# Changing how the first two x tiles and the first weight half reach TensorE in a gated mix of linear and local attention

## The chip, the cores and the metric

The kernel runs on one core of one Trainium2 chip. The metric is the device time of one execution, in microseconds (us); lower is better. A run also carries a mean granted TensorE clock. "Before" is the tuned kernel that the change starts from, "the changed kernel" is the result of the change. Four sets of runs are used, called A to D. In each set both kernels ran on the same chip; sets B, C and D were on three different chips.

## The reference

For x of 2048 rows by 1024 columns, the reference computes a gated sum of two attention blocks:

```
g = sigmoid((x * gate_w).sum(-1))
out = g * A(x) + (1 - g) * B(x)
A: linear attention, 32 heads of 32; phi(t) = where(t > 0, t + 1, exp(t)) + 1e-6 on q and k
B: sliding window of 8 keys, dilation 2, softmax; same shapes
each: qkv = x @ wqkv (1024 x 3072), output @ wo (1024 x 1024)
```

What matters here is only the first product: phi of x times the K columns of A's weights (1024 x 1024), done as two column halves of 512. It contracts over the 1024 columns of x, so TensorE needs x with columns on the partitions, that is, transposed.

## The kernel before

A tile of x is 128 rows (256 KB); there are 16. `xT` is x transposed, `xrow` x as it lies in memory. Tiles 0 and 1 are loaded plain and transposed on TensorE, because TensorE has nothing else to do then. Tiles 2 to 15 are transposed by the DMA crossbar on their way in. The first weight half (1 MB) comes in eight loads on the two issuing engines, SyncE and ScalarE.

```python
load_rows(nc.sync, 0, 1)
load_rows(nc.scalar, 1, 2)
WkA = [wpool.tile([P, KT, 512], BF16, name="WkA0", tag="wa")]
for kt in range(KT):                       # KT = 8
    (nc.scalar if kt % 2 else nc.sync).dma_start(out=WkA[0][:, kt, :], in_=A_wqkv[kt * P:(kt + 1) * P, D:D + 512])
for t in range(2, NB):                     # NB = 16
    nc.sync.dma_start_transpose(out=xT[:, :, t * P:(t + 1) * P], in_=rows(x, t * P, (t + 1) * P))
WkA += load_w("WkA", A_wqkv, D, "wa", only=(1,))
load_rows(nc.sync, 2, 4)
# ... (cut: other weights, constants)
def warm_up(n):
    warm = ps_1.tile([P, P], F32, name="warm", tag="p1")
    for i in range(n):
        nc.tensor.matmul(warm[:], lhsT=onesb[:], rhs=onesb[:], start=True, stop=True)

warm_up(28)
for t in range(2):
    tp = ps_1.tile([P, KT, P], BF16, name="xt_ps", tag="p1")
    for kt in range(KT):
        nc.tensor.transpose(out=tp[:, kt, :], in_=xrow[:, t, kt * P:(kt + 1) * P], identity=ident[:])
    nc.vector.tensor_copy(out=xT[:, 0:4, t * P:(t + 1) * P], in_=tp[:, 0:4, :])
    nc.scalar.copy(out=xT[:, 4:8, t * P:(t + 1) * P], in_=tp[:, 4:8, :])
warm_up(6)
# then tiles 0 and 1 together, 16 matmuls of 128x512, kt by kt; then tiles 2 to 15, 8 matmuls each
```

The warm-up matmuls compute nothing that is used. They keep TensorE busy so that its clock, halved at the start, is released early.

Of the kernel before, what the change touches and what calls it, by code (L numbers as in the profile page):

```python
# [10 lines left out]
BF16 = mybir.dt.bfloat16  # L11
F32 = mybir.dt.float32
PE = mybir.EngineType.PE
DVE = mybir.EngineType.DVE
P = 128
# [26 lines left out]
def kernel(  # L42
# [11 lines left out]
    nc = tc.nc  # L54
    S, D = A_x.shape[1:]
    assert D == 1024 and S == 2048

    x = A_x[0].rearrange("(m two) d -> two m d", two=2)
    out2 = out[0].rearrange("(m two) d -> two m d", two=2)

    def rows(ap, s0, s1):
        return ap[s0 // 1024, s0 % 1024:(s1 - 1) % 1024 + 1, :]
# [3 lines left out]
    KT = D // P  # L66
    NB = S // P
# [10 lines left out]
    big = ctx.enter_context(tc.tile_pool(name="big", bufs=1))  # L78
# [3 lines left out]
    def load_w(name, src, col0, tag, only=(0, 1)):  # L82
        halves = []
        for h in only:
            w = wpool.tile([P, KT, 512], BF16, name=f"{name}{h}", tag=tag)
            c0 = col0 + h * 512
            nc.sync.dma_start(out=w[:], in_=src[:, c0:c0 + 512].rearrange("(kt p) n -> p kt n", p=P))
            halves.append(w)
        return halves

    xT = big.tile([P, KT, S], BF16, name="xT", tag="xT")
    xrow = big.tile([P, NB, D], BF16, name="xrow", tag="vV")

    def load_rows(eng, t0, t1):
        eng.dma_start(out=xrow[:, t0:t1, :], in_=rows(x, t0 * P, t1 * P).rearrange("(t p) d -> p t d", p=P))

    load_rows(nc.sync, 0, 1)
    load_rows(nc.scalar, 1, 2)
    WkA = [wpool.tile([P, KT, 512], BF16, name="WkA0", tag="wa")]
    for kt in range(KT):  # L100
        (nc.scalar if kt % 2 else nc.sync).dma_start(out=WkA[0][:, kt, :], in_=A_wqkv[kt * P:(kt + 1) * P, D:D + 512])
    for t in range(2, NB):
        nc.sync.dma_start_transpose(out=xT[:, :, t * P:(t + 1) * P], in_=rows(x, t * P, (t + 1) * P))
    WkA += load_w("WkA", A_wqkv, D, "wa", only=(1,))
    load_rows(nc.sync, 2, 4)
    for t in range(4, NB, 4):
        load_rows(nc.sync, t, t + 4)
# [35 lines left out]
    def phi(dst, pj):  # L143
        e = work.tile([P, 512], F32, name="e", tag="e")
        nc.scalar.activation(out=e[:], in_=pj[:], func=ACT.Exp)  # L145
        nc.vector.tensor_scalar(out=e[:], in0=e[:], scalar1=1.0, scalar2=1e-6, op0=ALU.min, op1=ALU.add)  # L146
        nc.vector.scalar_tensor_tensor(out=dst, in0=pj[:], scalar=0.0, in1=e[:], op0=ALU.max, op1=ALU.add)

    with tc.manual_schedule(engines={PE}):

        with ExitStack() as s1:
            ps_1 = s1.enter_context(tc.tile_pool(name="ps_1", bufs=6, space=bass.MemoryType.PSUM))
            junk = s1.enter_context(tc.tile_pool(name="junk", bufs=1))


            def warm_up(n):
                warm = ps_1.tile([P, P], F32, name="warm", tag="p1")
                for i in range(n):
                    nc.tensor.matmul(warm[:], lhsT=onesb[:], rhs=onesb[:], start=True, stop=True)

            warm_up(28)
            for t in range(2):
                tp = ps_1.tile([P, KT, P], BF16, name="xt_ps", tag="p1")
                for kt in range(KT):
                    nc.tensor.transpose(out=tp[:, kt, :], in_=xrow[:, t, kt * P:(kt + 1) * P], identity=ident[:])  # L165
                nc.vector.tensor_copy(out=xT[:, 0:4, t * P:(t + 1) * P], in_=tp[:, 0:4, :])
                nc.scalar.copy(out=xT[:, 4:8, t * P:(t + 1) * P], in_=tp[:, 4:8, :])
            warm_up(6)

            s1.enter_context(tc.manual_schedule(engines={DVE}))  # L170
            pk = big.tile([P, NB, D], BF16, name="pk", tag="pkO")
            for half in range(2):
                for t0, n in [(0, 2)] + [(t, 1) for t in range(2, NB)]:
                    pj = [ps_1.tile([P, 512], F32, name="pk_ps", tag="p1") for _ in range(n)]
                    for kt in range(KT):
                        for i in range(n):
                            t = t0 + i
                            nc.tensor.matmul(pj[i][:], lhsT=xT[:, kt, t * P:(t + 1) * P], rhs=WkA[half][:, kt, :],  # L178
                                             start=(kt == 0), stop=(kt == KT - 1))
                    for i in range(n):  # L180
                        phi(pk[:, t0 + i, half * 512:(half + 1) * 512], pj[i])

            zacc = junk.tile([P, D], F32, name="zacc", tag="zacc")
            gw_row = junk.tile([P, D], BF16, name="gw_row", tag="gw")
# [12 lines left out]
            for half in range(2):  # L197
                g_ = kq.tile([P, KT, 512], BF16, name=f"G{half}", tag="kq")
                G.append(g_)
                for kt in range(KT):  # L200
                    pj = ps_1.tile([P, 512], F32, name="g_ps", tag="p1")
                    for t in range(NB):
                        nc.tensor.matmul(pj[:], lhsT=xrow[:, t, kt * P:(kt + 1) * P],  # L203
                                         rhs=pk[:, t, half * 512:(half + 1) * 512],
                                         start=(t == 0), stop=(t == NB - 1))
# [12 lines left out]
            for c in range(KT):  # L218
                kvp = ps_1.tile([P, P], F32, name="kv_ps", tag="p1")
                for kt in range(KT):  # L220
                    nc.tensor.matmul(kvp[:], lhsT=WvA[c // 4][:, kt, (c % 4) * P:(c % 4 + 1) * P],  # L221
                                     rhs=G[c // 4][:, kt, (c % 4) * P:(c % 4 + 1) * P],
                                     start=(kt == 0), stop=(kt == KT - 1))
                nc.vector.tensor_tensor(out=KVT[:, c, :], in0=kvp[:], in1=bdmask[:], op=ALU.mult)
            for half in range(2):
                zp = ps_1.tile([P, 512], F32, name="z_ps", tag="p1")
                for i in range(2):
                    nc.tensor.matmul(zp[:], lhsT=onesb[:], rhs=zhl[:, i, half * 512:(half + 1) * 512],  # L228
                                     start=(i == 0), stop=(i == 1))
# [300 lines left out]
```

## Time and profile before

| | before |
|---|---|
| median of 3 runs | 494.51 us (494.06 to 494.51) |
| span in the profile | 493.0 us |
| first projection matmul | 7.51 us |
| tile 2 starts | 12.39 us |
| tile 2 to the end | 480.6 us |

The first lines of the profile page give the span, and each engine's busy time, share of the span and instructions (PEld is TensorE's weight load):

```profile
span 493.0 us, 8254 instructions
...
PE 487.6 (99%) x3350; PEld 232.0 (47%) x3350; DVE 283.3 (57%) x550; ACT 181.9 (37%) x281; POOL 7.9 (2%) x28
```

TensorE is busy for all but 5.4 us. So a change at the kernel's head can gain time almost only by moving the moment at which TensorE's unbroken stream begins. The chain of waits of the first 20 us, in order of time (start, duration, what), shows what sets that moment:

```profile
...
0.80 4.34 DMA xrow<-in_A_x_dram
5.14 0.05 issue
5.19 1.89 PE xt_ps L165 x16
7.08 0.64 PE warm L159 x6
7.72 12.38 PE pk_ps L178 x51
```

The first 14 us of TensorE on the timeline (start, duration, engine, line, operation, what it writes and reads, count; in brackets the idle time before it and what ended it):

```profile
1.12 3.17 PE L159 MATMUL warm<-onesb 128*128 128x128 bf16 x28 [1.12 <-DVE onesb L117]
5.19 1.89 PE L165 MATMUL xt_ps<-ident,xrow 128*128 128x128 bf16 x16 [0.91 <-DMA xrow<-in_A_x_dram]
6.87 0.85 PE L159 MATMUL warm<-onesb 128*128 128x128 bf16 x6
7.51 6.76 PE L178 MATMUL pk_ps<-WkA_77,xT 128*128 128x512 bf16 x24
```

The warm-ups end at about 4.3 us, x tile 0 lands at 5.14 us, and the projection starts at 7.51 us. At full clock a 128x512 matmul starts every 216 ns. The first seven here start every 427 ns, because the clock is halved until 10.38 us.

A trap for the reader of profiles: the clock record begins with the first release. The table of windows therefore prints a clock of 1.00 for the time before 10.38 us, when the matmuls run at half speed. The matmuls' own spacing has to be read instead.

### The profile page before, as it was taken

What the parts mean: (1) busy time and instruction counts of PE and PEld (TensorE: products, weight loads), DVE (VectorE), ACT (ScalarE), POOL (GpSimd) and SP (SyncE); (2) the same over time, 40 slices, a digit from 0 to 9 for tenths busy, and PEclk for the clock granted to TensorE, in tenths of its full rate; (3) what the DMA queues carried; (4) which work ended last, traced back from release to release, by engine and by line L of the source; (5) the groups of instructions that cost most, each with busy time, mean ns of one, the idle gap of its engine ahead of it and who ended that gap; (6) DMA issues with size and microseconds to landing.
All of it is one profiled execution on the core that took longest, in us unless ns stands there. A gap on an engine that the chain in (4) does not pass through costs nothing.

```text
span 493.0 us, 8254 instructions
## 1 busy us (share of the span) xinstructions
PE 487.6 (99%) x3350; PEld 232.0 (47%) x3350; DVE 283.3 (57%) x550; ACT 181.9 (37%) x281; POOL 7.9 (2%) x28
## 2 busy tenths in 40 slices
PE   8999999999999999999999999999999999999997
PEld 5444444446444444444444545454544444444444
DVE  1766689941328999997476767676765397000000
ACT  1333311121543333332455655655655333112121
POOL 3000000000200000000000000000000000000000
PEclk9999999999999999999999999999999999999999
DMA  8999950000621222236011133111164832110101
GB/s 192 163 277 368 348 167 0 1 0 13 206 76 47 93 93 83 66 122 199 3 36 30 32 88 57 30 36 30 36 134 92 208 85 68 60 43 33 43 33 43
DMA packets 78293, 46.03 MB, mean 93 GB/s; under 512 B 51632, under 2 KB 72240, under 8 KB 78256
## 3 DMA queue, kind: packets, MB, share of 16 engines
q1 hardware_dynamic: 77536, 44.73, 33.6%
q10 hardware_dynamic: 720, 0.79, 0.6%
q8 instruction: 26, 0.43, 0.4%
q14 instruction: 11, 0.09, 0.1%
HBM read 21.23 MB, written 7.34 MB: 58 GB/s over the span
## 4 chain that ended last, share of the span: by engine, by line
PE 98%; DMA 1%; ACT 0%; issue 0%; ACTq 0%
PE kq_ps L339 23%; PE d_ps L458 21%; PE pk_ps L178 11%; PE p_ps L262 11%; PE g_ps L203 11%; PE p_ps L296 8%; PE q_ps L296 2%; DMA xrow<-in_A_x_dram 1%; PE kv_ps L221 1%; PE q_ps_4385 L458 1%; PE q_ps L458 1%; PE p_ps L251 1%; PE xt_ps L165 0%; PE q_ps_4266 L296 0%; PE q_ps_4165 L296 0%; PE z_ps L228 0%
## 5 line engine op out<-in xcount | busy, mean ns | idle before, releaser
L203 PE MATMUL g_ps<-pk,xrow 128*128 128x512 bf16 x256 | 55.4, 379 | 0.0
L146 DVE TENSOR_SCALAR e<-e 128x512 f32<-128x512 f32 x64 | 27.2, 424 | 39.9 <-ACT e L145 39.9
L463 ACT ACTIVATE osb<-d_ps,omg 128x512 bf16<-128x512 f32 (+1 forms) x31 | 20.9, 673 | 72.5 <-PE d_ps L458 64.2
L178 PEld LDWEIGHTS <-xT 128*128 128x128 bf16 x256 | 25.4, 99 | 31.0 <-issue 1.8
L458 PEld LDWEIGHTS <-OBT 128*128 128x128 bf16 x264 | 25.7, 98 | 29.2
L203 PEld LDWEIGHTS <-xrow 128*128 128x128 bf16 x256 | 25.0, 98 | 30.2
L262 PEld LDWEIGHTS <-xT 128*128 128x128 bf16 x256 | 25.0, 98 | 30.2
L296 PEld LDWEIGHTS <-xT 128*128 128x128 bf16 x256 | 24.2, 98 | 28.0
L378 DVE TENSOR_TENSOR PT_1893<-PT_1893,mask 128x672 bf16<-128x672 bf16 (+3 forms) x42 | 23.7, 571 | 18.1 <-ACT PT_1893 L376 17.7
L339 PE MATMUL kq_ps<-xT,WkB_1071 128*128 128x512 bf16 x128 | 32.9, 380 | 0.0
L339 PE MATMUL kq_ps<-xT,WqB_1876 128*128 128x512 bf16 x128 | 32.9, 379 | 0.0
L145 ACT ACTIVATE e<-pk_ps 128x512 f32<-128x512 f32 x32 | 18.9, 597 | 37.9 <-PE pk_ps L178 37.9
L339 PE MATMUL kq_ps<-xT,WkB_1069 128*128 128x512 bf16 x128 | 32.3, 379 | 0.0
L339 PE MATMUL kq_ps<-xT,WqB_1874 128*128 128x512 bf16 x128 | 32.2, 379 | 0.0
L378 DVE TENSOR_TENSOR PT_1894<-PT_1894,mask 128x672 bf16<-128x672 bf16 (+3 forms) x40 | 22.3, 565 | 16.8 <-ACT PT_1894 L376 16.5
L345 DVE CAST kqt<-kq_ps 128x512 bf16<-128x512 f32 x32 | 22.0, 687 | 16.5 <-PE kq_ps L339 16.5
L262 PE MATMUL p_ps<-WvB_114,xT 128*128 128x512 bf16 x128 | 30.9, 379 | 0.0
L262 PE MATMUL p_ps<-WvB_116,xT 128*128 128x512 bf16 x128 | 30.9, 379 | 0.0
L458 PEld LDWEIGHTS <-pqT_4443 128*128 128x128 bf16 x200 | 19.6, 98 | 22.1
L267 ACT CAST tmp<-p_ps 128x512 bf16<-128x512 f32 x32 | 18.8, 587 | 30.3 <-PE p_ps L262 30.3
L178 PE MATMUL pk_ps<-WkA_77,xT 128*128 128x512 bf16 x128 | 29.2, 392 | 0.0
L458 PE MATMUL d_ps<-WoB_4080,OBT 128*128 128x512 bf16 (+1 forms) x128 | 28.5, 366 | 0.0
(399 smaller groups left out, 673.6 us busy)
## 6 DMA issues: line engine op xcount, KB each, us to landing
out_dram<-osb SPq DMA_DIRECT2D x31, 128.0 KB, 1.9
xrow<-in_A_x_dram SPq DMA_DIRECT2D x3, 1024.0 KB, 12.0
pqd<-tmp SPq DMA_DIRECT2D x12, 256.0 KB, 2.0
V<-tmp SPq DMA_DIRECT2D x4, 264.0 KB, 2.5
WkA_100<-in_A_wqkv_dram SPq DMA_DIRECT2D x1, 1024.0 KB, 7.2
WvA_106<-in_A_wqkv_dram SPq DMA_DIRECT2D x1, 1024.0 KB, 14.6
WvA_108<-in_A_wqkv_dram SPq DMA_DIRECT2D x1, 1024.0 KB, 15.3
WoA_110<-in_A_wo_dram SPq DMA_DIRECT2D x1, 1024.0 KB, 13.1
```

The lines of the kernel that those rows point to most:

```text
L145: nc.scalar.activation(out=e[:], in_=pj[:], func=ACT.Exp)
L146: nc.vector.tensor_scalar(out=e[:], in0=e[:], scalar1=1.0, scalar2=1e-6, op0=ALU.min, op1=ALU.add)
L178: nc.tensor.matmul(pj[i][:], lhsT=xT[:, kt, t * P:(t + 1) * P], rhs=WkA[half][:, kt, :], start=(kt == 0), stop=(kt == KT - 1))
L203: nc.tensor.matmul(pj[:], lhsT=xrow[:, t, kt * P:(kt + 1) * P], rhs=pk[:, t, half * 512:(half + 1) * 512], start=(t == 0), stop=(t == NB - 1))
L262: nc.tensor.matmul(st["pj"][:], lhsT=xT[:, kt, t * P:(t + 1) * P], rhs=WvB[half][:, kt, :], start=(kt == 0), stop=(kt == KT - 1))
L267: nc.scalar.copy(out=v[:, half * 16:(half + 1) * 16, 0:Dh], in_=st["pj"][:].rearrange("p (h e) -> p h e", h=16))
L296: nc.tensor.matmul(st["pj"][:], lhsT=xT[:, kt, t * P:(t + 1) * P], rhs=WqA[half][:, kt, :], start=(kt == 0), stop=(kt == KT - 1))
L339: nc.tensor.matmul(st["pj"][:], lhsT=W[c // 4][:, kt, (c % 4) * P:(c % 4 + 1) * P], rhs=xT[:, kt, cols], start=(kt == 0), stop=(kt == KT - 1))
L345: nc.vector.tensor_copy(out=kqt[:, 1, cols], in_=st["pj"][:])
L378: nc.vector.tensor_tensor(out=ptv[:, hs], in0=ptv[:, hs], in1=m[:, None, :].broadcast_to([P, 2, W_]), op=ALU.mult)
L458: nc.tensor.matmul(st["ps"][:, 0:n], lhsT=lhsT, rhs=W[c0 // 512][:, c, c0 % 512:c0 % 512 + n], start=(side == 0 and c == 0), stop=(side == ...
L463: nc.scalar.activation(out=osb[:, 0:n], in_=st["ps"][:, 0:n], func=ACT.Copy, scale=omg[:, tb:tb + 1])
```

## The change

The intent is to start the projection earlier. x tile 0 comes by the crossbar, first on the queue, so that it needs neither TensorE transposes nor copies. The weights come as four quarters on the same queue, with x tile 1 plain between them. The matmuls are put in the order in which their data should arrive. The core of the diff, with lines cut and one line in brackets put for the lines that it names. `project` is one matmul of the projection, `transpose_rows` the eight transposes and two copies of one tile, `phi` the activation that follows:

```diff
-    load_rows(nc.sync, 0, 1)
-    load_rows(nc.scalar, 1, 2)
     WkA = [wpool.tile([P, KT, 512], BF16, name="WkA0", tag="wa")]
-    for kt in range(KT):
-        (nc.scalar if kt % 2 else nc.sync).dma_start(out=WkA[0][:, kt, :], in_=A_wqkv[kt * P:(kt + 1) * P, D:D + 512])
+    nc.sync.dma_start_transpose(out=xT[:, :, 0:P], in_=rows(x, 0, P))
+    for i in range(4):
+        if i == 1:
+            load_rows(nc.sync, 1, 2)
+        nc.sync.dma_start(out=WkA[0][:, 2 * i:2 * i + 2, :],
+                          in_=A_wqkv[2 * i * P:(2 * i + 2) * P, D:D + 512].rearrange("(kt p) n -> p kt n", p=P))
...
     WkA += load_w("WkA", A_wqkv, D, "wa", only=(1,))
+    load_rows(nc.sync, 0, 1)
     load_rows(nc.sync, 2, 4)
...
-            warm_up(28)
-            for t in range(2):
-                (transpose tile t on TensorE, copy it to xT)
-            warm_up(6)
+            warm_up(36)
+            first = [ps_1.tile([P, 512], F32, name="pk_ps", tag="p1") for _ in range(2)]
+            for t, kts in ((0, (0, 1)), ("T", 1), (0, (2, 3)), (1, (0, 1, 2, 3)), (0, (4, 5)), (1, (4, 5)),
+                           (0, (6, 7)), (1, (6, 7))):
+                if t == "T":
+                    transpose_rows(kts)
+                    continue
+                for kt in kts:
+                    project(first[t], t, kt, 0)
+                if kts[-1] == KT - 1:
+                    phi(pk[:, t, 0:512], first[t])
```

From tile 2 on, every computing engine has the same instructions in the same order; SyncE has one load more, the rows of tile 0.

## The prediction

> **What bounds the kernel now.** TensorE is busy 487.6 of 493.0 us (engine table), and the chain of waits is 98% TensorE. From 7.51 us to the end its stream waits for no load; the timeline shows one 128x512 matmul start per 216 ns. So the change can touch only the first 12.4 us, when tiles 0 and 1 of the first projection end (tile 2 starts at 12.39 us). By the timeline they hold: 28 warm-up matmuls from 1.12 to 4.28; 0.91 us idle until the plain load of x tile 0 lands (5.14 us); 16 TensorE transposes and 6 warm-ups at 107 ns (2.3 us); 16 matmuls from 7.51 us, seven at 427 ns because the clock is halved until 10.38 us, nine at 216 ns.
>
> **The clock.** The trace's clock record is halved up to 10.38 us and again from 491.66 us: 481.28 us apart, 141.0 times 3.413 us. That agrees with the free-running 3413 ns window of the Trainium skill ("TensorE: Matmul & The Clock Gate", Part 1). A boundary then lay at 6.97 us; the window before it held the 0.91 us gap and did not release the clock.
>
> **What the change does.**
> - Removes from TensorE 8 transposes and 6 warm-ups after the data (1.5 us at 107 ns), and one PSUM-to-SBUF copy pair (0.42 and 0.58 us). Adds 8 warm-ups before the data, free.
> - Moves: x tile 0 comes by crossbar, first. Issuing a transpose takes 1.31 us of SyncE; landing came 3.9 us after issue at best, under load; issued at 0.8 us, I expect 4.5 to 5.2 us. Weight quarters and x tile 1 follow on one queue, 256 KB each, about 0.7 us each at the 380 GB/s the trace reached: near 5.2 (quarter 0), 5.8 (x1), 6.5, 7.2, 7.9 us. Before, weight rows 5 and 7 landed only at 10.39 and 10.87 us, as their ScalarE issue waited for semaphores until 5.83 us.
> - Crossbar tiles 2 to 15 should flow from about 8 us at 1.4 to 1.55 us each, under the 1.73 us TensorE needs per tile. The second weight half, landing at 34.64 us before (needed near 36.5), should land about 33 us; needed then at 34: little slack.
> - x rows of tile 0 again, 256 KB, needed only at 64 us: free. All other instruction orders are unchanged.
>
> **Sum.** Projection starts near 5.1 us. If gaps stay below about 0.6 us, the clock is released near 7 us: two matmuls and eight transposes halved to 6.9 us, then 14 matmuls at 216 ns: tile 2 starts at 9.9 us instead of 12.4, 2.5 us gained. If the clock is released only at 10.38 us, tile 2 starts at 11.7: 0.7 us. Weight arrival (7.9 us plus four matmuls) caps the gain at about 3.5 us. I allow 0.3 us for later waits. Prediction: gain about 2.0 us, 492.5 us; 8 in 10 between 491.0 and 494.2. Faster by over 2% 0.01, within 2% 0.98, slower by over 2% 0.01.
>
> **Signs.** Right: first projection matmul at 4.8 to 5.5 us; full clock before 8 us; tile 2 starts at 9 to 10.5 us; no wait over 0.3 us at tiles 2 to 15 or the second weight half; from there the same durations, shifted. Wrong: crossbar landing after 6 us, clock still halved at 10 us, or later crossbar or weight waits that give the gain back.
>
> **What would make it wrong.** A slow first crossbar load; window phase differing between runs; the second weight half late.

## The result, and the profile after

Set A: the changed kernel took 493.27 us (median of 6, 492.6 to 496.03), before 494.51 us (median of 6, 494.06 to 495.1). The ratio is 0.9981, with a 95% interval of 0.9957 to 1.0006: the same. Ratios here are the mean time of one kernel's fast runs over that of the other's of the same rounds, so they are not quite the ratio of the medians quoted. The scatter grew from 1.0 to 3.4 us (to 1.3 us without the one run at 496.03 us).

The profile after, same views. The page's first lines:

```profile
span 490.9 us, 8176 instructions
...
PE 480.6 (98%) x3283; PEld 230.1 (47%) x3344; DVE 283.3 (58%) x549; ACT 181.2 (37%) x280; POOL 7.9 (2%) x28
```

TensorE's busy time is understated here: matmul records are missing, about one in fifty (x3283 against x3344 weight loads), and on the timeline each leaves a gap of two matmul steps, about 430 ns. It must not be read as idling. The chain of the first 20 us:

```profile
...
0.80 1.33 SPq L98
...
2.19 0.57 SPq L102
...
2.81 0.46 SPq L95
...
3.31 4.21 DMA WkA_75<-in_A_wqkv_dram
...
7.56 0.83 PE pk_ps L161 x3
...
8.45 10.74 PE pk_ps L161 x49
...
```

And TensorE's first 14 us:

```profile
1.12 3.46 PE L167 MATMUL warm<-onesb 128*128 128x128 bf16 x36 [1.12 <-DVE onesb L120]
6.11 0.59 PE L161 MATMUL pk_ps<-WkA_75,xT 128*128 128x512 bf16 x2 [1.52 <-DMA WkA_75<-in_A_wqkv_dram]
6.87 0.62 PE L172 MATMUL xt_ps<-ident,xrow 128*128 128x128 bf16 x8 [0.17 <-DMA xrow<-in_A_x_dram]
7.56 6.66 PE L161 MATMUL pk_ps<-WkA_75,xT 128*128 128x512 bf16 x29
```

The chain now begins with the crossbar load's issue on SyncE (1.33 us, line 98). The next two issues stand behind it, then weight quarter 1, issued at 3.31 us and landed at 7.52 us. TensorE idles 1.52 us before quarter 0. Then 14 matmuls run at 216 ns, and tile 2 starts at 10.60 us instead of 12.39: 1.78 us gained. This is a favourable pair: the profiled run of the changed kernel (492.60 us) is the fastest of its six, and that of before (494.82 us) lies above the median. In this profile the clock was released at 3.85 us, before the first projection matmul. In the profile of before it was released at 10.38 us. So two things differ between the two profiles, the loads and the clock. The experiments separate them.

From tile 2 to the end of the span the two profiles need 480.62 and 480.29 us. Nothing in between moved; the last 0.3 us are explained in the last section.

### The profile page after: what moved, and what is told of

The parts are those of the page before. It is cut to its first block, busy times and chain, and to the rows that moved or that the text cites. A ratio compares the mean times of both kernels' runs of the same rounds, so it can differ in the third digit from the quotient of the medians.

```text
span 490.9 us, 8176 instructions
## 1 busy us (share of the span) xinstructions
PE 480.6 (98%) x3283; PEld 230.1 (47%) x3344; DVE 283.3 (58%) x549; ACT 181.2 (37%) x280; POOL 7.9 (2%) x28
## 4 chain that ended last, share of the span: by engine, by line
PE 97%; issue 1%; DMA 1%; SPq 0%; DVE 0%; ACT 0%; ACTq 0%
PE kq_ps L353 23%; PE d_ps L472 21%; PE g_ps L217 11%; PE p_ps L276 11%; PE pk_ps L161 11%; PE p_ps L310 8%; PE q_ps L310 2%; DMA WkA_75<-in_A_wqkv_dram 1%; PE kv_ps L235 1%; PE q_ps_4372 L472 1%; PE p_ps L265 1%; PE q_ps L472 1%; PE q_ps_4253 L310 0%; PE q_ps_4152 L310 0%; SPq L98 0%
## 5 line engine op out<-in xcount | busy, mean ns | idle before, releaser
L353 PE MATMUL kq_ps<-xT,WqB_1863 128*128 128x512 bf16 x120 | 31.8, 379 | 1.0 <-issue 0.6
L353 PE MATMUL kq_ps<-xT,WqB_1861 128*128 128x512 bf16 x124 | 31.7, 379 | 0.7 <-issue 0.5
L392 DVE TENSOR_TENSOR PT_1881<-PT_1881,mask 128x672 bf16<-128x672 bf16 (+3 forms) x40 | 22.3, 565 | 16.8 <-ACT PT_1881 L390 16.5
L353 PE MATMUL kq_ps<-xT,WkB_1058 128*128 128x512 bf16 x122 | 31.6, 379 | 0.2
L359 DVE CAST kqt<-kq_ps 128x512 bf16<-128x512 f32 x32 | 22.0, 687 | 16.5 <-PE kq_ps L353 16.5
L353 PE MATMUL kq_ps<-xT,WkB_1056 128*128 128x512 bf16 x120 | 30.7, 379 | 0.4 <-issue 0.2
L161 PE MATMUL pk_ps<-WkA_75,xT 128*128 128x512 bf16 x125 | 27.8, 379 | 1.8 <-DMA WkA_75<-in_A_wqkv_dram 1.5
```

The lines of the kernel that those rows point to most:

```text
L161: nc.tensor.matmul(pj[:], lhsT=xT[:, kt, t * P:(t + 1) * P], rhs=WkA[half][:, kt, :], start=(kt == 0), stop=(kt == KT - 1))
L353: nc.tensor.matmul(st["pj"][:], lhsT=W[c // 4][:, kt, (c % 4) * P:(c % 4 + 1) * P], rhs=xT[:, kt, cols], start=(kt == 0), stop=(kt == KT - 1))
L359: nc.vector.tensor_copy(out=kqt[:, 1, cols], in_=st["pj"][:])
L392: nc.vector.tensor_tensor(out=ptv[:, hs], in0=ptv[:, hs], in1=m[:, None, :].broadcast_to([P, 2, W_]), op=ALU.mult)
```

## The experiments

Two theories. **A (loads):** the head is as long as the loads make it. **B (clock phase):** the clock is released, and can be halved again, at the boundaries of a free-running window; where they fall differs from run to run, so gaps between warm-ups and data decide. They were told apart by profiles of the same kernel at other phases, by filling the gaps, and by changing the loads alone.

The landing times in the tables were read from the trace (the last of the sixteen semaphore increments of a load); "tile 2" is the start of its first matmul. Landings of one load order differ between sets by up to 0.9 us (quarter 3 of the changed kernel: 8.97 us in set A, 9.87 us in set B).

### Set B: the change again, gaps filled, weights in quarters

Run `a_repeat` is the changed kernel unaltered.

> The changed kernel again, unaltered. In its first profile the clock was released at 3.85 us, quarter 0 landed at 6.07 us (estimated 5.2 before) and tile 2 started at 10.60 us; in the profile of before the release was at 10.38 us. Theory A (loads): TensorE waits for loads, so tile 2 starts between 10.4 and 10.9 us in any profile, and the runs scatter no more than those of before (about 1 us). Theory B (clock phase): the release falls where the free-running window falls; a profile of a bad phase shows release between 9 and 10.5 us and tile 2 at 11.4 to 12.2 us, and the runs scatter by 1 to 1.5 us or more; the mean gain over before is then about 1 us, not 2.

Run `a_warm48`:

```diff
-            warm_up(36)
+            warm_up(48)
```

> The changed kernel with 48 instead of 36 warm-up matmuls, so that at half clock they last until about 6.2 us, when quarter 0 lands. Theory A: no change, within 0.2 us of the changed kernel. Theory B: the release can no longer slip to 9 us or later; mean 0.3 to 0.8 us below the changed kernel and a narrower spread; every profile has the release before 7.3 us and tile 2 at 10.4 to 11.2 us.

Run `b_warm38`, from the kernel before:

```diff
-            warm_up(28)
+            warm_up(38)
```

> The kernel before with 38 instead of 28 warm-up matmuls, so that at half clock they last until 5.19 us, when x tile 0 has landed: the 0.91 us gap is filled. Theory B: release before 7.3 us in the profile instead of 10.38 us; then the late weight rows (10.39 and 10.87 us) bind and tile 2 starts at 11.2 to 11.7 us, 0.3 to 1.0 us faster than before on average. Theory A: nothing, within 0.2 us of before.

Run `b_quarters`, from the kernel before:

```diff
-    for kt in range(KT):
-        (nc.scalar if kt % 2 else nc.sync).dma_start(out=WkA[0][:, kt, :], in_=A_wqkv[kt * P:(kt + 1) * P, D:D + 512])
+    for i in range(4):
+        (nc.scalar if i % 2 else nc.sync).dma_start(
+            out=WkA[0][:, 2 * i:2 * i + 2, :],
+            in_=A_wqkv[2 * i * P:(2 * i + 2) * P, D:D + 512].rearrange("(kt p) n -> p kt n", p=P))
```

> The kernel before with its first weight half loaded as four quarters of two rows of tiles each, alternating between the two issuing engines, instead of eight eighths: six loads instead of ten, so none waits for a semaphore. Both x tiles still plain and both transposed on TensorE. Theory A (late weight rows and waits in the queue are what the change cures): weights all landed by about 7 us instead of 10.87, and crossbar tiles earlier by 1 us or more; but if the clock is released only near 10.4 us tile 2 still starts at 12.4 us and the gain is near 0. With the clock released early tile 2 starts at 9.7 to 10.5 us and the gain is about 2 us. So Theory B expects a mean gain between 0 and 1 us with a spread of about 2 us.

Measured, beside before at 494.25 us (median of 11, 493.5 to 495.13):

| run | median (lowest to highest), us | ratio to before (95%) | release in its profile | last weights land | tile 2 |
|---|---|---|---|---|---|
| a_repeat | 494.86 (493.06 to 495.22) | 1.0008 (0.9996 to 1.0021) | about 10.3 us | 9.87 us | 12.38 us |
| a_warm48 | 493.43 (493.37 to 493.61) | 0.9986 (0.9974 to 0.9998) | about 5.7 us | 9.74 us | 11.38 us |
| b_warm38 | 493.74 (493.42 to 494.73) | 0.9990 (0.9977 to 1.0002) | 4.22 us | 11.38 us | 12.21 us |
| b_quarters | 492.37 (492.15 to 494.3) | 0.9973 (0.9960 to 0.9986) | 5.42 us | 8.27 us | 9.98 us |

The same changed kernel gave no gain here, where Theory B expected a mean gain of about 1 us; the scatter, 2.16 us, is as it expected. Its profile has the late release. TensorE's first 14 us of `a_repeat`:

```profile
1.12 4.02 PE L167 MATMUL warm<-onesb 128*128 128x128 bf16 x36 [1.12 <-DVE onesb L120]
6.40 1.01 PE L161 MATMUL pk_ps<-WkA,xT 128*128 128x512 bf16 x2 [1.26 <-DMA WkA<-in_A_wqkv_dram]
7.20 1.06 PE L172 MATMUL xt_ps<-ident,xrow 128*128 128x128 bf16 x8
8.46 5.80 PE L161 MATMUL pk_ps<-WkA,xT 128*128 128x512 bf16 x22 [0.20 <-DMA WkA<-in_A_wqkv_dram]
```

All 36 warm-ups run at half clock here (4.02 us against 3.46). The eight transposes take 1.06 us against 0.62, and the matmuls keep a spacing of 427 ns until about 10.3 us. Tile 2 starts at 12.38 us, where before had it. There is no clock record in the profiles of `a_repeat`, `a_warm48` and `a_warm0`; their releases are read from the spacing and marked "about".

With 48 warm-ups the five runs of `a_warm48` lie within 0.24 us, where the unaltered kernel's six lie within 2.16 us, and their mean is 1.13 us lower. This was more than the 0.3 to 0.8 us expected, while tile 2, at 11.38 us, was later than the 10.4 to 11.2 us expected. Theory A expected no difference, so it is refuted as the whole story. But the loads vary too: `a_warm48` runs all its projection matmuls at full clock, and still starts tile 2 0.78 us later than the profile of set A, because quarter 1 landed at 8.32 us instead of 7.52.

`b_warm38` shows that something else holds before too, which may be why it scatters less. Its clock was released at 4.22 us, yet tile 2 starts at 12.21 us, later than the 11.2 to 11.7 us expected. The waits of its first 14 us (engine and line, what it waited for, total us, times, longest) and its timeline:

```profile
...
PE pk_ps L178 <- DMA WkA<-in_A_wqkv_dram: 1.8, 1, 1.8
...
```

```profile
...
5.38 1.07 PE L165 MATMUL xt_ps<-ident,xrow 128*128 128x128 bf16 x16 [0.51 <-DMA xrow<-in_A_x_dram]
6.29 0.50 PE L159 MATMUL warm<-onesb 128*128 128x128 bf16 x6
6.62 2.46 PE L178 MATMUL pk_ps<-WkA,xT 128*128 128x512 bf16 x10
10.92 3.40 PE L178 MATMUL pk_ps<-WkA,xT 128*128 128x512 bf16 x15 [1.83 <-DMA WkA<-in_A_wqkv_dram]
```

TensorE, now early, waits 1.83 us for row tile 5 of the weights (the sixth of the eight loads), which lands at 10.87 us; row tile 7 lands at 11.38 us. Before makes ten loads at the start. In the trace the loads share eight semaphores, and from the ninth on each waits until an earlier load with the same semaphore has landed. The ScalarE issues of row tiles 5 and 7 therefore went out only at 6.03 and 6.43 us, the first of them just after row tile 0 had landed at 6.01 us. In before, the late clock and the late weights lie side by side: taking away the late clock alone gained 0.4 us of mean, which is not clear of noise (the interval holds 1). The profiled run is also the slowest of the five (494.73 us). The spans of the other four, 491.5 to 491.8 us, less the 480.62 us that its load list needs from tile 2 to the end, put tile 2 at about 10.9 to 11.2 us (an estimate). So the wait of 1.83 us is not that of a typical run. By the same estimate the eleven runs of before in this set start tile 2 at 11.0 to 12.5 us, so the profile of before, at 12.39 us, is a late one as well.

`b_quarters` takes away the late weights alone: six loads, no wait for a semaphore, the last quarter landed at 8.27 us (about 7 us had been expected). From the first projection matmul on, TensorE's timeline is one piece:

```profile
...
6.38 7.86 PE L180 MATMUL pk_ps<-WkA,xT 128*128 128x512 bf16 x35
```

Its median gain is 1.88 us, with a spread of 2.15 us, since two of its six runs (493.65 and 494.3 us) are well above the other four (492.15 to 492.48 us), as Theory B expects of a kernel whose gap is still open. The mean gain, 1.4 us, is above the 0 to 1 us expected. So one part of the change, without the crossbar load and without the new order, beats the whole change on this chip.

### Set C: both causes away, and the crossbar load by itself

Run `b_quarters38` is `b_quarters` with `warm_up(38)` for `warm_up(28)`.

> The kernel before with quarters on both issuing engines and 38 warm-up matmuls: both causes taken away, no crossbar for tile 0. If the loads and the clock phase together are the whole story, every run is like the early-release runs of the quarters alone: 492.0 to 492.6 us, spread under 0.5 us, release before 7.3 us, tile 2 at 9.9 to 10.5 us: about 2 us faster than before and 1 us faster than the changed kernel with 48 warm-ups. If the crossbar load of tile 0 were needed for the gain, it would stay within 0.5 us of before.

Run `a_plain`, from the changed kernel:

```diff
-    nc.sync.dma_start_transpose(out=xT[:, :, 0:P], in_=rows(x, 0, P))
+    load_rows(nc.sync, 0, 1)
...
-    load_rows(nc.sync, 0, 1)
     load_rows(nc.sync, 2, 4)
...
-            warm_up(36)
+            warm_up(34)
-            for t, kts in ((0, (0, 1)), ("T", 1), ...
+            for t, kts in (("T", 0), (0, (0, 1)), ("T", 1), ...
```

> The changed kernel with x tile 0 loaded plain in the crossbar's place and transposed on TensorE (8 transposes more, 34 warm-ups), all else kept: one queue, quarters, matmuls in order of arrival. If the crossbar load is what makes the first matmul late (its issue takes 1.33 us and everything queues behind it), quarter 0 lands about 1 us earlier than in the changed kernel (5.0 to 5.4 us instead of 6.07 to 6.56), quarter 3 by 8.5 us instead of 8.97 to 9.87, and the time is 0.5 to 1.2 us below the changed kernel with 48 warm-ups. If the crossbar saves more on TensorE than it costs in the queue, it is slower than that kernel by about 0.5 us.

Run `a_q0first`, from the changed kernel:

```diff
-    nc.sync.dma_start_transpose(out=xT[:, :, 0:P], in_=rows(x, 0, P))
     for i in range(4):
         if i == 1:
+            nc.sync.dma_start_transpose(out=xT[:, :, 0:P], in_=rows(x, 0, P))
             load_rows(nc.sync, 1, 2)
...
-            warm_up(36)
+            warm_up(42)
```

> The changed kernel with weight quarter 0 issued ahead of the crossbar load of x tile 0, and 42 warm-ups; all else kept. If the first load's issue time is what counts (0.6 us for a quarter against 1.33 us for a crossbar load), data flow while the crossbar load is still being issued: quarter 0 lands by 4.5 us, x tile 0 by 5.3 us, the first projection matmul starts at 5.0 to 5.5 us instead of 6.1 to 6.6, and the last quarter lands 0.3 to 0.8 us earlier. Time 0.3 to 0.9 us below the changed kernel with 48 warm-ups. If a crossbar load amid plain loads flows badly (the rival), x tile 0 lands after 6 us and nothing is gained.

Run `a_warm0` is the changed kernel without its line `warm_up(36)`.

> The changed kernel without warm-up matmuls: same loads, but the clock can be released only after TensorE has worked from about 6.1 us, so between 8.8 and 12.4 us. Clock theory: tile 2 at 11.6 to 13.3 us in the profile, times 493.9 to 495.6 us, mean about 1.3 us above the changed kernel with 48 warm-ups; as slow as the slowest runs of the changed kernel or slower. If the clock played no part (loads only), the time is that of the changed kernel within 0.3 us.

Measured, beside before at 494.62 us (median of 11, 493.81 to 496.78; two of its runs, 496.42 and 496.78 us, raise its mean, so that ratios come out about 0.0006 lower than medians would give):

| run | median (lowest to highest), us | ratio (95%) | x tile 0 lands | quarter 0 | quarter 3 | release | tile 2 |
|---|---|---|---|---|---|---|---|
| b_quarters38 | 492.67 (492.11 to 493.1) | 0.9953 (0.9935 to 0.9970) | 4.94 us | 6.32 us | 8.58 us | 6.48 us | 10.61 us |
| a_plain | 492.26 (492.0 to 492.67) | 0.9946 (0.9927 to 0.9964) | 3.47 us | 4.83 us | 8.69 us | 6.06 us | 10.47 us |
| a_q0first | 492.71 (492.3 to 493.08) | 0.9954 (0.9937 to 0.9971) | 6.09 us | 4.22 us | 9.17 us | 4.00 us | 10.72 us |
| a_warm0 | 494.80 (493.76 to 496.45) | 0.9998 (0.9978 to 1.0019) | 4.17 us | 5.65 us | 9.52 us | about 9.5 us | 11.77 us |

- `b_quarters38` has no run above 493.1 us and gains 1.95 us in the median without any crossbar load for tile 0. It did not quite reach the 492.0 to 492.6 us and tile 2 by 10.5 us expected: at its phase the 16 transposes still ran at half clock (release at 6.48 us), and the first projection matmul came at 7.02 us.
- `a_plain` puts a plain load in the crossbar's place. Quarter 0 lands at 4.83 us, where the five profiles of the changed kernel's load order with warm-ups (sets A, B and D) have 5.96 to 6.56 us. Part of that is issue: quarter 0 is issued at 1.26 us instead of 2.19 us. TensorE did not use this lead: its first projection matmul came at 6.30 us, after the transposes and copies of x tile 0. What it did use is quarter 1, which landed at 7.29 us, against 7.52 to 8.42 us in those five profiles.
- In `a_q0first` the expectation failed. Quarter 0 landed at 4.22 us as expected, but the crossbar tile behind it landed at 6.09 us, 4.8 us after its issue, where first in the queue it took 3.4 us. The first projection matmul stayed at 6.14 us. So the rival reading given for this run holds for the landing. "Nothing is gained" is not borne out: the run is 1.9 us faster than before and level with `b_quarters38`. Nor is it shown that a crossbar load suffers more than any second load would: the plain load behind a plain one in `a_plain` took 3.56 us from issue to landing, where the first took 2.67 us.
- `a_warm0` has the same loads and no warm-ups. It is as slow as before. The clock theory's range for the profile (11.6 to 13.3 us) holds; two of its six runs, 493.76 and 496.45 us, are outside the times expected, and the slower one is unexplained. No run with 48 warm-ups was made on this chip, so the differences from it that were expected in this set are not tested here.

### Set D: the main comparisons on one chip, and a version from the findings

Runs `a_again`, `a_warm48_2` and `a_plain_2` repeat the changed kernel, its variant with 48 warm-ups and the plain variant.

> The changed kernel again, as the yardstick on the same chip for the next three. So far its twelve runs lie between 492.6 and 496.0 us, mean ratio to before 0.998 and 1.001. Clock theory: again a scatter of over 1 us and a mean within 1.3 us of before; in the profile either release before 6 us with tile 2 near 10.6 to 11.4 us, or after 9 us with tile 2 above 11.4 us.

> The changed kernel with 48 warm-ups again, on the same chip as the plain variant. Clock theory: spread under 0.6 us, mean below the changed kernel's by 0.3 to 1.3 us, release before 7.3 us.

> x tile 0 plain and transposed on TensorE, otherwise the changed kernel, again: now on one chip with the 48 warm-ups. If the crossbar load at the head of the queue costs more than the eight transposes it saves, it is 0.4 to 1.2 us faster than the 48 warm-ups; if not, equal within 0.3 us or slower.

Run `one_queue`, from the kernel before:

```diff
-    load_rows(nc.scalar, 1, 2)
+    load_rows(nc.sync, 1, 2)
...
-    for kt in range(KT):
-        (nc.scalar if kt % 2 else nc.sync).dma_start(out=WkA[0][:, kt, :], in_=A_wqkv[kt * P:(kt + 1) * P, D:D + 512])
+    for i in range(4):
+        nc.sync.dma_start(out=WkA[0][:, 2 * i:2 * i + 2, :],
+                          in_=A_wqkv[2 * i * P:(2 * i + 2) * P, D:D + 512].rearrange("(kt p) n -> p kt n", p=P))
...
-            warm_up(28)
+            warm_up(24)
             for t in range(2):
+                if t:
+                    warm_up(4)
```

> The kernel before, with everything that the runs so far point to: both x tiles plain and first, then the four weight quarters, all on one queue (no wait for a semaphore), both tiles transposed on TensorE, and warm-ups put into the gaps (24, 4 and 6 of them) so that the clock has no gap of over 0.5 us. x tiles should land at 3.5 and 4.9 us, quarters at 6.2, 7.0, 7.7 and 8.5 us; 16 matmuls at 216 ns from quarter 0 on: tile 2 at 9.7 to 10.1 us; 491.6 to 492.2 us, spread under 0.6 us, 0.2 to 0.6 us below the plain variant. If the release comes late in some runs, those are at 493 us and more.

Measured, beside before at 494.23 us (median of 9, 493.39 to 494.82):

| run | median (lowest to highest), us | ratio (95%) | quarter 0 lands | quarter 3 | clock in the profile | tile 2 |
|---|---|---|---|---|---|---|
| a_again | 494.79 (494.64 to 495.0) | 1.0013 (1.0000 to 1.0025) | 5.96 us | 9.67 us | full at 5.28, half at 8.69, full at 12.11 us | 12.98 us |
| a_warm48_2 | 493.46 (493.1 to 493.81) | 0.9985 (0.9973 to 0.9998) | 6.32 us | 9.39 us | full at 3.96 us | 11.02 us |
| a_plain_2 | 492.62 (492.33 to 493.1) | 0.9968 (0.9954 to 0.9981) | 4.61 us | 9.16 us | full at 7.06 us | 10.83 us |
| one_queue | 492.10 (491.63 to 492.36) | 0.9958 (0.9945 to 0.9970) | 6.26 us | 8.57 us | full at 6.50 us | 9.92 us |

The profile of `a_again` shows a third outcome for the changed kernel, one that the prediction did not have. The clock is released at 5.28 us and halved again at 8.69 us. The windows between those boundaries (window, length, busy us and instructions of PE, PEld, DVE, ACT and POOL, then granted clock, DMA share, GB/s):

```profile
1.87:5.28 3.41, 3.27 (x31) 3.11 (x30) 0.00 (x0) 0.21 (x1) 3.05 (x15) 1.00 0.80 193
5.28:8.69 3.41, 1.63 (x12) 0.79 (x12) 0.42 (x1) 0.58 (x1) 0.00 (x0) 1.00 1.01 273
8.69:12.11 3.42, 3.20 (x8) 1.17 (x8) 0.00 (x0) 0.00 (x0) 0.00 (x0) 0.50 1.08 214
...
```

In the middle window TensorE waits for quarter 0, for x tile 1 and for quarter 1, and is busy for 1.63 of 3.41 us. The next window runs at half clock, in the middle of the projection: there are only 8 recorded matmuls in it. TensorE's timeline:

```profile
...
6.01 0.59 PE L161 MATMUL pk_ps<-WkA,xT 128*128 128x512 bf16 x2 [0.86 <-DMA WkA<-in_A_wqkv_dram]
6.91 0.62 PE L172 MATMUL xt_ps<-ident,xrow 128*128 128x128 bf16 x8 [0.31 <-DMA xrow<-in_A_x_dram]
8.28 1.06 PE L161 MATMUL pk_ps<-WkA,xT 128*128 128x512 bf16 x3 [0.75 <-DMA WkA<-in_A_wqkv_dram]
9.56 4.67 PE L161 MATMUL pk_ps<-WkA,xT 128*128 128x512 bf16 x15 [0.22 <-issue]
```

Tile 2 starts at 12.98 us, 0.6 us later than before. All five runs of `a_again`, which lie within 0.36 us where a scatter of over 1 us was expected, have a mean granted clock of 0.996 or 0.997, and so have four of the six runs of `a_repeat` (494.69 to 495.22 us), but none of set A. One window at half clock costs 3.41 / 2 us of 493, which is 0.0035: just that clock. Of the unaltered kernel's 17 runs in sets A, B and D, nine carry this mark, at 494.64 to 495.22 us, all above every median of before. None of the runs of `a_warm48`, `a_warm48_2`, `a_plain` or `one_queue` carries it. Two runs of before do, 496.42 and 496.78 us in set C. A listed clock of 1.0 proves less: the profiled runs without a clock record (`a_repeat`, `a_warm48`, `a_warm0`) are listed at 1.0 too.

`one_queue` has no crossbar load at the head, no wait for a semaphore, and small gaps. Its chain and its timeline:

```profile
...
1.12 2.74 PE warm L160 x24
3.86 0.85 PE xt_ps L168 x8
4.71 0.43 PE warm L160 x4
5.14 0.85 PE xt_ps L168 x8
5.99 0.64 PE warm L160 x6
6.63 0.43 PE pk_ps L181 x2
...
7.12 7.07 PE pk_ps L181 x32
```

```profile
...
3.65 1.06 PE L168 MATMUL xt_ps<-ident,xrow 128*128 128x128 bf16 x8
4.51 0.63 PE L160 MATMUL warm<-onesb 128*128 128x128 bf16 x4
4.93 1.06 PE L168 MATMUL xt_ps<-ident,xrow 128*128 128x128 bf16 x8
5.79 0.85 PE L160 MATMUL warm<-onesb 128*128 128x128 bf16 x6
6.43 7.76 PE L181 MATMUL pk_ps<-WkA,xT 128*128 128x512 bf16 x34
```

From 1.12 us on the chain holds TensorE alone: no load ends a wait that counts. The landings came within 0.2 us of those expected for it. It is 2.13 us faster than before and 2.69 us faster than the changed kernel, in medians on one chip, and correct. Its spread, 0.73 us, is a little over the 0.6 expected, and its slowest run, 492.36 us, above the 492.2. One part of it was not tested by itself: with all loads on one queue x tile 0 lands at 3.55 us, with loads issued on both engines at 4.88 to 5.34 us (on one chip, 3.47 us in `a_plain` against 4.94 us in `b_quarters38`).

The 48 warm-ups again lower the changed kernel's mean, by 1.36 us (0.3 to 1.3 expected), but with a spread of 0.71 us (under 0.6 expected). The plain variant is 0.84 us faster than they are on this chip, as was expected (0.4 to 1.2 us) if the crossbar load costs more than it saves. The two profiles show only part of this: tile 2 starts 0.19 us earlier, with quarter 1 at 7.75 instead of 7.96 us, and the part after tile 2 is 0.28 us shorter. The profiled run of the plain variant is the slowest of its five.

Across all profiles, tile 2 to the end of the span takes 480.27 to 480.68 us: the whole difference between these kernels arises before tile 2, apart from 0.35 us at the end and 0.4 us that `a_warm48_2` lost in a wait for a crossbar tile at 16.5 us. Outside the span there is a little more: the times exceed the spans by 1.94 us in before and 1.72 us in the changed kernel (means of set B); why is not known.

## Why the prediction was right or wrong

By the result it was right: 493.27 us is inside 491.0 to 494.2, and "within 2%" had 0.98. That was partly luck. Two of its signs fail even in the profile of set A, which is that of the fastest run: the first projection matmul at 6.11 us (4.8 to 5.5 expected) and tile 2 at 10.60 us (9 to 10.5). The release came at 3.85 us, not near 7, and 0.3 us were gained at the kernel's end, where nothing was forecast. The gain of 2.0 us was too large, and the range did not hold for the sets that followed: their medians, 494.86 and 494.79 us, are above 494.2. Taken together, the mean change was -0.9, +0.3 and +0.6 us in sets A, B and D: no gain that can be relied on.

- *TensorE-bound after 7.5 us, so only the head can move.* Right but for the end of the kernel: tile 2 to the end is constant to 0.35 us.
- *"Projection starts near 5.1 us."* Wrong by about 1 us: 6.11, 6.40 and 6.01 us in the three profiles of the unaltered change. The step that failed is the landing of weight quarter 0. x tile 0 by crossbar landed at 4.20 us, even earlier than the 4.5 to 5.2 expected, but quarter 0 landed at 6.07, 6.36 and 5.96 us instead of 5.2. I had added 0.7 us of transfer to the crossbar's landing. In the trace, quarter 0 is issued only at 2.19 us, and takes 3.8 to 4.2 us from issue to landing.
- *Quarters every 0.7 us, the last at 7.9 us.* The spacing was right in set A (0.70 to 0.75 us), the last landing wrong by 1 us (8.97 us). In sets B and D it was wrong by almost 2 us (9.87, 9.67 us): there quarter 1 landed 1.4 us behind x tile 1, and why is not known.
- *"If gaps stay below about 0.6 us, the clock is released near 7 us."* The condition was named, and it is the step that failed: the gap before quarter 0 is 0.9 to 1.5 us. Then three outcomes came up. Release at 3.85 us (set A, 1.8 us gained). Release at about 10.3 us (`a_repeat`, nothing gained; the prediction's second branch, with tile 2 at 12.38 us instead of 11.7). And release followed by a second halving (`a_again`, 0.6 us lost), which the prediction did not have.
- *"Window phase differing between runs"* stood among the things that would make it wrong, and did so, together with the late quarters. The runs with 48 warm-ups show its size: 1.13 and 1.36 us of mean.
- *Later crossbar tiles and the second weight half in time.* Right in set A: no such wait, half 1 landed at 33.48 us. In `a_warm48_2` one crossbar tile cost 0.4 us, so the slack is thin.
- The hidden point of the comparison: before had two causes of about the same length side by side, late clock (10.38 us) and late weights (10.87 us). The profile of before shows only the first, since no wait for weights was left. `b_warm38` made the second visible. On average the weights cost more: taking them away alone gained 1.4 us of mean (`b_quarters`), taking away the late clock alone 0.4 us (`b_warm38`).

What stays open: why all five runs of `a_again` fell into the second halving while none did in set A. Phases of timed runs are not recorded. The runs at 496.03 us (set A) and 496.45 us (`a_warm0`), listed at a clock of 1.0, are unexplained too. The two slow runs of before in set C are listed at 0.997 and are 1.80 and 2.16 us slower than its median, most of which a window at half clock (1.71 us) would explain; no profile shows one.

## What to carry to other kernels

Before taking time out of a kernel's head, list every cause that ends at about the same moment, including those that leave no wait in the profile, and check in the issue list whether some loads go out late for want of a free semaphore. Judge a change of a few us at the head by several runs on several chips, and look at the scatter and the granted clock: if the clock's release hangs on where a free-running window falls, fill the gaps with warm-ups up to the moment of the slowest landing. Here that took 1.1 and 1.4 us off the mean; it narrowed the scatter in set B only. Try a plain load in place of one that is slow to issue at the head of a queue that everything else stands behind: here that variant was 0.84 us faster. Check where the profiled run lies among the timed ones before reading a difference of 1 us from two profiles.

## What the Trainium skill lacked or had wrong

- **"TensorE: Matmul & The Clock Gate", Part 1**, gives a free-running window of 3413 ns, and the runs agree: in before, release and the last halving are 481.28 us apart, 141.0 windows. Its table lets the clock fall back after an idle window; here it was halved after a window in which TensorE was busy for 1.63 of 3.41 us (`a_again`). The same page, under "A second HAM failure mode: psum-queue depth-cycling", does tell of a clock that falls back after frequent short idling, but without a share. The table calls for a busy window to release the clock and gives no share: windows with 2.73 us (after, 0.43 to 3.85 us) and 2.77 us (`b_quarters`, 2.00 to 5.42 us) released it, those with 2.51 us (before, 3.55 to 6.97 us) and 2.53 us (`a_plain_2`, 0.24 to 3.65 us) did not. The share that keeps the clock can't be given from these runs: 1.72 us kept it in the profile after, but so did 1.58 us in `b_warm38` (7.63 to 11.04 us), so the busy time that the profile models is not all that counts.
- **"DMA: Bandwidth & Descriptors", Anatomy of one DMA**, gives about 2.0 us fixed cost plus transfer, measured for loads issued from GpSimd. A plain 256 KB load at the head of the one queue landed 2.7 us after its issue on SyncE (`a_plain`, 0.80 to 3.47 us), which agrees with an estimate of the page's 2.0 us and 0.7 us of transfer at the 380 GB/s that the trace of before reached. With loads on both engines it took 4.34 us (before, 0.80 to 5.14 us).
- **The same page, Rules for kernel authors**, says that a transpose beside ordinary DMAs needs nothing. That is about correctness. For time, the skill has bandwidths of transposing loads, but no page that was read has that a 256 KB crossbar load took 3.4 us first in the queue and 4.8 us behind one plain 256 KB load (`a_q0first`), or that its issue occupied SyncE for 1.33 us, where that of a plain load took 0.40 us (`a_plain`).
- No page that was read has this: at the end of the kernel SyncE waits for the load semaphores one after the other, about 63 ns each. In before the last output's semaphore is first in that row, and four more steps follow its landing; in the changed kernel it is last. That is 0.29 us against 0.04 us from its wait to the drain, and most of the 0.35 us by which tile 2 to the end is shorter. Where the last output stands follows the number of loads: `b_warm38`, with the loads of before, also needs 480.62 us from tile 2 to the end, the changed kernel's load list 480.27 to 480.37 us (but for the wait in `a_warm48_2`), and `b_quarters`, `a_plain` and `one_queue` 480.39 or 480.40 us.
